# Second layer: the second product takes its first two factors in chunks 0 to 3, then 4 to 7

## The chip, the cores and the metric

The kernel runs on one core of a Trainium2 chip. The metric is the device time of one execution in microseconds. Engines are named as in the profile: PE (matrix products, with its weight loads as PEld), DVE (vector), ACT (scalar), POOL, and SP, which issues most DMAs.

## The reference

Attention with two softmaxes that are taken apart (no product of q and k), then two layers of the same shape:

```python
kv = einsum('bhsd,bhse->bhde', softmax_over_s(k), v)
x = einsum('bhsd,bhde->bhse', softmax_over_d(q), kv)     # as 4608 tokens x 512
h = x @ w_in;  x = square(maximum(h, 0)) @ w_out          # first layer, 512 -> 2048 -> 512
h = x @ w_in2; g = where(h > 0, h, exp(minimum(h, 0)) - 1)
out = g @ w_out2                                          # second layer, 512 -> 2048 -> 512
```

Everything is fp32. Each factor of a product is taken as the sum of a high and a low half (fp32r), and three of the four products of halves are computed.

## The kernel before, in words

Attention and first layer fill the first 849 us and are the same in both kernels. The change lies in `second_layer` (lines 1014 to 1077).

The second layer goes over five blocks of tokens, three with twice 512 tokens and two with twice 384 (`SIZES`); they are called wide and narrow here, and numbered 0 to 4. Both of its products are done by a scheme that replaces eight products of quarters by seven ("units" 0 to 6) of sums and differences of quarters. A block has two parts.

First product (line 871): 56 small products of six matmuls, for eight chunks m of two times 128 hidden features and seven units i each. `ORDER` (line 845) gives each a step number from 0 to 56, and after the product of a step the work put at that step is issued. Three accumulators A, B and C (`CHAIN`) hold the partial sums of a chunk; units 0, 2, 4 and 5 add into A in turn, and between them ACT (`keep_part`, line 896, and 908) or DVE (`h_part`, line 910) reads it out. Then the ELU of a row of quarters runs in five pieces: `elu_1` to `elu_3` on ACT (lines 916, 922, 927), `elu_4` and `elu_5` on DVE (931, 935). Results lie in `g2`, quarters B11, B12, B21, B22; two chunks m make one chunk pair k = 0 to 3.

Second product (line 976): 56 units u, taken two by two as pairs q = 0 to 27. `SECOND` (line 839) names the factor i and chunk j of each unit; chunks 2k and 2k+1 need the quarters of chunk pair k. Factor 4 is T3 = B22 - B12, factor 3 is T1 = B12 - B11, which is computed in place of B12. `t2_sum` (line 949, DVE) makes these differences; `d_split` (lines 956 and 957) makes a pair's high half dh on ACT and its low half dl on DVE, into three buffers each. `d_mm` then multiplies 128 x 128 pieces of dh and dl with w, in the order dh, dl, dh: 24 matmuls a pair in a wide block, 18 in a narrow one.

Each engine does its instructions in the order in which they are issued here. Splits 0, 1 and 2 are issued during the first product, split q+2 after pair q for q from 1. `put(("d", q), ...)` puts work behind pair q of the second product, `put(step, ...)` behind a step of the first. The last chunk's ELU falls on pairs 0 to 3. The weights come through a ring of 11 tiles (`w2_load`), loaded by SP in the order of use.

```python
            for q in range(NU // 2):
                d_mm(n, 2 * q)
                d_mm(n, 2 * q + 1)
                run(steps.get(("d", q), ()))
                if 0 < q < NU // 2 - 2:
                    d_split(n, q + 2)
```

Of the kernel before, what the change touches and what calls it, by code (L numbers as in the profile page):

```python
# [20 lines left out]
def tile_attention_moe_moe2(  # L21
# [714 lines left out]
    def u_out(t, i, side, half, block, m):  # L736

        o = parts_y[i][m]
        nc.vector.tensor_tensor(o, o, accs[side, m], op=ALU.add)
        nc.gpsimd.dma_start(x2d[block][2 * half + m], o)  # L740
# [95 lines left out]

    SECOND = [(i, j) for js in (range(6), range(6, 8)) for i in (4, 3) for j in js]
    SECOND += [(i, j) for i in (0, 6, 2, 1, 5) for j in range(NG)]  # L840
    SIDE = {i: (side, new) for i, side, new in SEVEN}

# [4 lines left out]
    def stream():  # L847
        for n in range(len(SIZES)):
            for _, m, i in ORDER:
                yield w2s[m][:, i]  # L850
            for i, j in SECOND:
                yield w3s[j][:, i]
# [33 lines left out]
    def take(n, m, i):  # L886
        c = CHAIN[i], m
        begin = i in (0, 1, 3)
        if begin:
            ps, tag = (psh, "ph") if i == 0 else (psa, "att")  # L890
            acc[c] = ps.tile([P, SIZES[n]], F32, tag=tag, name=f"p{n}_{m}_{i}")
        product(n, i, acc[c], begin)
# [46 lines left out]
    def quarter(name, k):  # L939
        if name == "T3":  # L940
            return g2["T3", k]
        r, side = {"B11": (0, 0), "B12": (0, 1), "B21": (1, 0), "B22": (1, 1), "T1": (0, 1), "T2": (0, 0), "T4": (1, 0)}[name]
        return g2[r, k][:, :, side]
# [7 lines left out]
    def d_split(n, q):  # L951
        i, j = SECOND[2 * q]
        x = quarter(UNITS[i], j // 2)
        hi = shifted("gh", f"dh{n}_{q}", n)
        lo = shifted("gl", f"dl{n}_{q}", n)
        nc.scalar.activation(hi, x, AF.Copy)  # L956
        nc.vector.tensor_tensor(lo, x, f32(hi), op=ALU.subtract)  # L957
        ops["d", q] = hi, lo
# [7 lines left out]
    def d_mm(n, u):  # L966
        i, j = SECOND[u]
        side, new = SIDE[i]
        w, (hi, lo) = ring.pop(0), ops["d", u // 2]
        for b, row, count in pieces2(n):  # L970
            if new and j == 0:
                y2[side, b] = psy.tile([P, count * HW], F32, tag=f"y{2 * side + b}", name=f"y2_{n}_{i}_{b}")
            for a in range(count):
                at = slice(row + a * P, row + (a + 1) * P)
                for s, x in ((0, hi), (0, lo), (1, hi)):
                    nc.tensor.matmul(  # L976
                        y2[side, b][:, a * HW : (a + 1) * HW],
                        x[:, u % 2, at],
                        w[:, s],
                        start=(new and (j, s, a) == (0, 0, 0) and x is hi),  # L980
                        stop=(j == NG - 1 and s == 1),
                        skip_group_check=True,
                    )
        w2_load()
# [16 lines left out]
    def d_out(n, i, side, half, to):  # L1001

        o = kept[i]
        for b, row, count in pieces2(n):
            c = slice(b * DM, b * DM + count * HW)
            nc.vector.tensor_tensor(o[:, c], o[:, c], y2[side, b], op=ALU.add)
            at = START[n] + to * SIZES[n] + row
            queue = nc.scalar if n == len(SIZES) - 1 and i == 4 and b else nc.sync
            queue.dma_start(
                out[at : at + count * P, half * HW : (half + 1) * HW].rearrange("(a p) c -> p a c", p=P),  # L1010
                o[:, c].rearrange("p (a c) -> p a c", c=HW),
            )

    def second_layer():


        nonlocal pool2
        for m in range(2):
            u_out(NB - 2, 4, 0, 1, NB - 2, m)
        early2.tile([P, 56], F32, tag="even", name="even")  # L1020
        layer_pool.__exit__(None, None, None)
        square_pool.__exit__(None, None, None)
        pool2 = ctx.enter_context(tc.tile_pool(name="pool2", bufs=1, reuse_waits="tile"))
        last = len(SIZES) - 1
        for n in range(last + 1):
            steps = {}

            def put(key, f, *a):
                steps.setdefault(key, []).append((f, (n, *a)))

            evict = {
                0: (keep_part, 0), 3: (keep_part, 3), 2: (keep_part, 2), 1: (h_part, 0, 0, 1, 0),
                6: (h_part, 0, 1, 6, 2), 4: (h_part, 1, 1, 4, 3), 5: (h_part, 1, 0, 5, None),
            }
            for at, m, i in ORDER:
                put(at, evict[i][0], m, *evict[i][1:])
            if n:
                put(1, lambda n: d_out(n - 1, 4, 0, 1, 0))
            for m in range(NG):
                for x, (to, f, r) in enumerate((  # L1040
                    (6, elu_1, 0), (7, elu_2, 0), (8, elu_3, 0), (9, elu_4, 0), (10, elu_5, 0), (10, elu_1, 1),
                    (11, elu_2, 1), (12, elu_3, 1), (13, elu_4, 1), (14, elu_5, 1),
                )):
                    put(7 * m + to if m < NG - 1 else ("d", (0, 0, 0, 1, 1, 1, 2, 2, 3, 3)[x]) if x else 56, f, m, r)
            for k in range(3):
                put(14 * k + 22, t2_sum, "T3", k)
                put(14 * k + 25 if k < 2 else ("d", 0), t2_sum, "T1", k)
            put(30, d_split, 0)
            put(39, d_split, 1)
            put(54, d_split, 2)  # L1050
            for q, f, *a in (
                (4, t2_sum, "T3", 3), (4, t2_sum, "T1", 3),
                (6, d_keep, 4, 0, "e"), (8, d_v), (10, t2_sum, "T2", 0), (11, t2_sum, "T2", 1),
                (12, d_keep, 0, 0, "g"), (12, t2_sum, "T2", 2), (13, t2_sum, "T2", 3), (16, d_keep, 6, 1, "g"),
                (19, t2_sum, "T4", 0), (20, d_out, 6, 0, 0, 1), (21, d_out, "v", 0, 1, 1), (22, t2_sum, "T4", 1),
                (23, t2_sum, "T4", 2), (24, t2_sum, "T4", 3), (25, d_out, 0, 1, 0, 0),
            ):
                put(("d", q), f, *a)
            if n < last:
                for q, f, a in (  # L1060
                    (6, x2_sum, "T3"), (7, x2_sum, "T1"), (9, x2_split, 0), (14, x2_sum, "T2"), (15, x2_split, 1),
                    (16, x2_split, 6), (17, x2_split, 2), (18, x2_split, 3), (25, x2_sum, "T4"), (26, x2_split, 4),
                    (27, x2_split, 5),
                ):
                    steps.setdefault(("d", q), []).append((f, (n + 1, a)))
                for k, (side, h) in enumerate(((0, 0), (1, 0), (1, 1), (0, 1))):
                    steps.setdefault(35 + 2 * k, []).append((x2_load, (n + 1, h, side)))
            for at, m, i in ORDER:
                take(n, m, i)
                run(steps.get(at, ()))  # L1070
# [6 lines that stand above are left out]
        d_out(last, 4, 0, 1, 0)  # L1077
# [6 lines left out]
    def run(steps):  # L1084
        for f, a in steps:
            f(*a)
# [3 lines left out]
    with tc.manual_schedule():  # L1090
# [107 lines left out]
        for t in range(NB):  # L1198
# [40 lines left out]
            if right:  # L1239
                steps = pair_steps(t - 1, final)  # L1240
                for u in range(NU):
                    unit(t - 1, u)
        second_layer()


# [45 lines left out]
```

## Time and profile before

| | |
|---|---|
| median of 3 runs | 1565.22 us (1564.33 to 1568.18) |
| the profiled execution | 1564.8 us, its span 1563.0 us |
| PE busy | 1534.6 us, 98% of the span |
| DVE, ACT busy | 1230.0 us (79%), 1018.9 us (65%) |
| POOL busy | 122.9 us (8%) |
| mean granted clock of PE | 0.999 of 2.4 GHz |

The span is what the trace covers. Times in the trace are microseconds from its start. A busy PE alone says that the time is PE's; the waits of PE, one by one, and the chain of work that ended last say where another engine sets it.

### The profile page before, as it was taken

The numbers are of one execution on the slowest core, as the hardware profiler recorded it, in microseconds if no ns is written. First come the engines' busy times: TensorE is split into PE (matmuls) and PEld (weight loads), VectorE is DVE, ScalarE is ACT, GpSimd is POOL, SyncE is SP. The second block draws the span as 40 slices with busy tenths as digits, with TensorE's granted clock in tenths as the row PEclk, the third lists the DMA queues.
The fourth block names the chain that finished last, engine by engine and source line by source line (L and its number), as shares of the span: only waits on it lengthen the run. The fifth ranks groups of instructions, "written<-read, shape, count | busy, mean of one in ns | idle before, by whom it ended". The sixth has DMA issues, their size and how long they took to land.

```text
span 1563.0 us, 25532 instructions
## 1 busy us (share of the span) xinstructions
PE 1534.6 (98%) x9046; PEld 1324.2 (85%) x9046; DVE 1230.0 (79%) x1807; ACT 1018.9 (65%) x1636; POOL 122.9 (8%) x194
## 2 busy tenths in 40 slices
PE   6999999999999999999999999999999999999998
PEld 4777787887878787787888889988998899999998
DVE  7998687887778887786687788678877886887885
ACT  7886655567565765656564885388538853864863
POOL 0001220032001410022201000000000000000000
PEclk9999999999999999999999999999999999999999
DMA  9867566867576775755686786767687768888876
GB/s 250 250 175 234 203 242 192 276 222 242 180 242 228 268 260 150 251 184 183 210 280 212 195 246 180 241 196 244 182 240 195 233 181 243 280 259 280 262 238 206
DMA packets 201343, 352.99 MB, mean 226 GB/s; under 512 B 20224, under 2 KB 67328, under 8 KB 201216
## 3 DMA queue, kind: packets, MB, share of 16 engines
q1 hardware_dynamic: 186672, 304.03, 64.6%
q0 software_dynamic: 14400, 47.20, 7.6%
q8 instruction: 73, 1.20, 0.3%
q14 instruction: 54, 0.44, 0.1%
q10 hardware_dynamic: 144, 0.13, 0.0%
HBM read 288.36 MB, written 62.91 MB: 225 GB/s over the span
## 4 chain that ended last, share of the span: by engine, by line
PE 79%; DVE 12%; ACT 3%; issue 2%; DMA 1%; SPq 0%; DVEq 0%; ACTq 0%
PE p L871 21%; PE y L976 18%; PE p L710 16%; PE ph L593 7%; PE ph L595 7%; PE ph L594 7%; DVE dl L957 2%; PE px L427 1%; DVE ul L698 1%; PE pk L307 1%; DVE g L935 1%; PE pt L399 1%; ACT dh L956 1%; DVE t L931 1%; DMA w<-w1s 1%
## 5 line engine op out<-in xcount | busy, mean ns | idle before, releaser
L976 PE MATMUL y<-w,dh 128*128 128x256 f32 x2016 | 359.2, 281 | 0.0
L871 PE MATMUL p<-x2h,w 128*128 128x512 f32 (+1 forms) x1120 | 321.5, 367 | 0.0
L976 PEld LDWEIGHTS y<-w,dh 128*128 128x128 f32 x2016 | 309.8, 189 | 0.1
L976 PE MATMUL y<-w,dl 128*128 128x256 f32 x1008 | 285.3, 283 | 2.9 <-DVE dl L957 2.5
L710 PE MATMUL p<-uh,w 128*128 128x512 f32 x896 | 282.7, 392 | 0.1
L593 PE MATMUL ph<-xh,wi0h 128*128 128x512 f32 x576 | 229.6, 399 | 0.1
L871 PEld LDWEIGHTS p<-x2h,w 128*128 128x128 f32 x1120 | 207.1, 188 | 26.0
L595 PE MATMUL ph<-xh,wi0l 128*128 128x512 f32 x576 | 225.4, 391 | 2.7 <-DVE wi0l L149 2.7
L594 PE MATMUL ph<-xl,wi0h 128*128 128x512 f32 x576 | 225.1, 391 | 1.3 <-DVE xl L506 1.3
L871 PE MATMUL p<-x2l,w 128*128 128x512 f32 (+1 forms) x560 | 205.7, 367 | 0.0
L710 PEld LDWEIGHTS p<-uh,w 128*128 128x128 f32 x896 | 168.3, 188 | 36.7 <-issue 1.5
L976 PEld LDWEIGHTS y<-w,dl 128*128 128x128 f32 x1008 | 189.8, 188 | 5.8 <-DVE dl L957 5.3
L956 ACT ACTIVATE dh<-g 128x1024 fp32r<-128x1024 f32 (+1 forms) x120 | 115.8, 973 | 101.3 <-PE y L976 100.1
L697 ACT ACTIVATE uh<-B 128x512 fp32r<-128x512 f32 x192 | 120.4, 631 | 93.4 <-PE p L710 69.2
L710 PE MATMUL p<-ul,w 128*128 128x512 f32 x448 | 176.5, 394 | 1.8 <-DVE ul L698 1.4
L957 DVE TENSOR_TENSOR dl<-g,dh 128x1024 fp32r<-128x1024 f32 (+1 forms) x120 | 133.8, 1115 | 42.2 <-ACT dh L956 41.8
L698 DVE TENSOR_TENSOR ul<-B,uh 128x512 fp32r<-128x512 f32 x192 | 129.6, 688 | 46.5 <-ACT uh L697 45.9
L602 ACT ACTIVATE B<-ph 128x512 f32<-128x512 f32 x128 | 76.2, 596 | 119.9 <-PE ph L595 116.2
L593 PEld LDWEIGHTS ph<-xh,wi0h 128*128 128x128 f32 x576 | 109.2, 190 | 28.2 <-issue 3.9
L595 PEld LDWEIGHTS ph<-xh,wi0l 128*128 128x128 f32 x576 | 108.3, 188 | 26.5 <-DVE wi0l L149 3.5
L594 PEld LDWEIGHTS ph<-xl,wi0h 128*128 128x128 f32 x576 | 108.5, 188 | 23.4 <-DVE xl L506 2.3
L871 PEld LDWEIGHTS p<-x2l,w 128*128 128x128 f32 x560 | 105.2, 188 | 13.0
(141 smaller groups left out, 2287.2 us busy)
## 6 DMA issues: line engine op xcount, KB each, us to landing
w<-w2s SPq DMA_DIRECT2D x280, 256.0 KB, 3.2
w<-w3s SPq DMA_DIRECT2D x280, 256.0 KB, 3.0
w<-w1s SPq DMA_DIRECT2D x224, 256.0 KB, 3.6
raw_wo<-wo_dram SPq DMA_DIRECT2D x32, 512.0 KB, 4.2
ks<-k_dram SPq DMA_DIRECT2D x32, 320.0 KB, 4.5
vr<-v_dram SPq DMA_DIRECT2D x32, 320.0 KB, 5.4
kt<-kt_dram SPq DMA_DIRECT2D x32, 288.0 KB, 4.0
q<-q_dram SPq DMA_DIRECT2D x36, 256.0 KB, 5.0
```

The source lines that it names most:

```text
L307: nc.tensor.matmul(pk[j * D : (j + 1) * D], ks[:, c, j * D : (j + 1) * D], vr[:, c, j * (D + 1) : (j + 1) * (D + 1)], start=(c == 0), stop ...
L593: nc.tensor.matmul(ph, hi[:, c], xh[p], start=(p == 0), stop=False)
L594: nc.tensor.matmul(ph, hi[:, c], xl[p], start=False, stop=False)
L595: nc.tensor.matmul(ph, lo[:, c], xh[p], start=False, stop=(p == NP - 1))
L602: nc.scalar.activation(g, ph, AF.Relu)
L697: nc.scalar.activation(hi, x, AF.Copy)
L698: nc.vector.tensor_tensor(lo, x, f32(hi), op=ALU.subtract)
L710: nc.tensor.matmul(accs[side, m], w[:, s, m], x, start=(new and (j, s) == (0, 0) and x is hi), stop=(j == NG - 1 and s == 1), skip_group_c ...
L871: nc.tensor.matmul(acc, w[:, s, c], x[:, k], start=(begin and (k, s) == (0, 0) and x is hi), stop=((k, s) == (1, 1)), skip_group_check=not ...
L956: nc.scalar.activation(hi, x, AF.Copy)
L957: nc.vector.tensor_tensor(lo, x, f32(hi), op=ALU.subtract)
L976: nc.tensor.matmul(y2[side, b][:, a * HW : (a + 1) * HW], x[:, u % 2, at], w[:, s], start=(new and (j, s, a) == (0, 0, 0) and x is hi), st ...
```

## The change

`SECOND` gives another order of the pairs. Before: T3 of k = 0, 1, 2 (pairs 0 to 2), T1 of k = 0, 1, 2 (pairs 3 to 5), T3 of k = 3, T1 of k = 3 (pairs 6, 7). After: T3 of k = 0, 1 (pairs 0, 1), T1 of k = 0, 1 (pairs 2, 3), T3 of k = 2, 3 (pairs 4, 5), T1 of k = 2, 3 (pairs 6, 7). The differences and the third split are issued at other steps.

```diff
-    SECOND = [(i, j) for js in (range(6), range(6, 8)) for i in (4, 3) for j in js]
+    SECOND = [(i, j) for js in (range(4), range(4, 8)) for i in (4, 3) for j in js]
...
             for k in range(3):
-                put(14 * k + 22, t2_sum, "T3", k)
-                put(14 * k + 25 if k < 2 else ("d", 0), t2_sum, "T1", k)
+                put(14 * k + 22 if k < 2 else ("d", 1), t2_sum, "T3", k)
+                put(14 * k + 25 if k < 2 else ("d", 3), t2_sum, "T1", k)
             put(30, d_split, 0)
             put(39, d_split, 1)
-            put(54, d_split, 2)
+            put(47, d_split, 2)
             for q, f, *a in (
-                (4, t2_sum, "T3", 3), (4, t2_sum, "T1", 3),
+                (3, t2_sum, "T3", 3), (4, t2_sum, "T1", 3),
```

The order on DVE in block 0, steps 47 to 51, before. In the names dl_2 is the low half of split 2, g the quarters, p the accumulators of the first product (p_6_0 is A of chunk 6), t either a piece of the ELU or, as t_0_2 and t_0_3, T3 of k = 2 and 3 of block 0; the last number only tells buffers apart.

```order
L910 TENSOR_TENSOR g_0_3_9416<-k_6_2_9402,p_6_3_9372 128x512
L910 TENSOR_TENSOR g_0_3_9417<-k_6_3_9381,p_6_0_9358 128x512
L931 SCALAR_TENSOR_TENSOR t_5_1_9419<-e_5_1_9405,t_5_1_9419 128x1024
L935 SCALAR_TENSOR_TENSOR g_0_2_9234<-g_0_2_9234,t_5_1_9419 128x1024
L949 TENSOR_TENSOR t_0_2_9469<-g_0_2_9234,g_0_2_9233 128x1024
L931 SCALAR_TENSOR_TENSOR t_6_0_9455<-e_6_0_9441,t_6_0_9455 128x1024
```

The same steps on DVE after the change:

```order
L910 TENSOR_TENSOR g_0_3_9416<-k_6_2_9402,p_6_3_9372 128x512
L957 TENSOR_TENSOR dl_2_9432<-g_0_0_8895,dh_2_9431 128x1024
L910 TENSOR_TENSOR g_0_3_9417<-k_6_3_9381,p_6_0_9358 128x512
L931 SCALAR_TENSOR_TENSOR t_5_1_9419<-e_5_1_9405,t_5_1_9419 128x1024
L935 SCALAR_TENSOR_TENSOR g_0_2_9234<-g_0_2_9234,t_5_1_9419 128x1024
L931 SCALAR_TENSOR_TENSOR t_6_0_9459<-e_6_0_9445,t_6_0_9459 128x1024
```

Split 2, now of T1 of k = 0, stands ahead of the eviction of p_6_0 at step 48; T3 of k = 2 has left.

The order on DVE in block 0 behind pairs 1 to 5 of the second product, before. Here g_0_2_9233 as the only name of an L949 is T1 of k = 2, and g_0_3_9416 T1 of k = 3.

```order
L957 TENSOR_TENSOR dl_3_9609<-g_0_0_8895,dh_3_9608 128x1024
L957 TENSOR_TENSOR dl_4_9644<-g_0_1_9058,dh_4_9643 128x1024
L931 SCALAR_TENSOR_TENSOR t_7_1_9640<-e_7_1_9606,t_7_1_9640 128x1024
L935 SCALAR_TENSOR_TENSOR g_0_3_9417<-g_0_3_9417,t_7_1_9640 128x1024
L957 TENSOR_TENSOR dl_5_9680<-g_0_2_9233,dh_5_9679 128x1024
L949 TENSOR_TENSOR t_0_3_9711<-g_0_3_9417,g_0_3_9416 128x1024
L949 TENSOR_TENSOR g_0_3_9416<-g_0_3_9416 128x2x512
L957 TENSOR_TENSOR dl_6_9715<-t_0_3_9711,dh_6_9714 128x1024
L957 TENSOR_TENSOR dl_7_9747<-g_0_3_9416,dh_7_9746 128x1024
```

The same place on DVE after the change:

```order
L949 TENSOR_TENSOR t_0_2_9605<-g_0_2_9234,g_0_2_9233 128x1024
L957 TENSOR_TENSOR dl_3_9608<-g_0_1_9058,dh_3_9607 128x1024
L957 TENSOR_TENSOR dl_4_9645<-t_0_2_9605,dh_4_9644 128x1024
L931 SCALAR_TENSOR_TENSOR t_7_1_9641<-e_7_1_9603,t_7_1_9641 128x1024
L935 SCALAR_TENSOR_TENSOR g_0_3_9417<-g_0_3_9417,t_7_1_9641 128x1024
L949 TENSOR_TENSOR g_0_2_9233<-g_0_2_9233 128x2x512
L949 TENSOR_TENSOR t_0_3_9679<-g_0_3_9417,g_0_3_9416 128x1024
L957 TENSOR_TENSOR dl_5_9682<-t_0_3_9679,dh_5_9681 128x1024
L949 TENSOR_TENSOR g_0_3_9416<-g_0_3_9416 128x2x512
L957 TENSOR_TENSOR dl_6_9715<-g_0_2_9233,dh_6_9714 128x1024
L957 TENSOR_TENSOR dl_7_9747<-g_0_3_9416,dh_7_9746 128x1024
```

T3 of k = 3 is followed by its own split, which is now split 5 and no longer split 6; T1 of k = 2 stands in the place of the old split 5, and T3 of k = 2 ahead of split 3.

## Rows read from the trace of the kernel before

**Rows 1.** The page's busy times: engine, busy us, share of the span, instructions.
```profile
PE 1534.6 (98%) x9046; PEld 1324.2 (85%) x9046; DVE 1230.0 (79%) x1807; ACT 1018.9 (65%) x1636; POOL 122.9 (8%) x194
```
**Rows 2.** Chain that ended last, pieces in order of time: start, length in us.
```profile
943.52 62.82 PE y L976 x527
...
1006.34 70.75 PE p L871 x312
...
1319.79 54.10 PE p L871 x312
```
**Rows 3.** Engines by stretch: length, busy us (instructions) each; PE clock, DMA share, GB/s.
```profile
920.00:944.00 24.00, 23.50 (x175) 22.31 (x174) 20.66 (x20) 16.33 (x17) 0.00 (x0) 1.00 0.70 188
```
**Rows 4.** Waits of PEld from 920 us to the end: us, times, longest.
```profile
PEld y L976 <- DVE dl L957: 5.3, 12, 0.7
```
**Rows 5.** DVE in order of time, block 0: start, us, line, out<-in [idle before, releaser].
```profile
914.98 0.69 DVE L910 TENSOR_TENSOR g<-k,p 128x512 f32<-128x512 f32 x1 [0.48 <-PE p L871]
...
925.13 1.23 DVE L957 TENSOR_TENSOR dl<-t,dh 128x1024 fp32r<-128x1024 f32 x1 [1.30 <-ACT dh L956]
...
932.80 1.22 DVE L957 TENSOR_TENSOR dl<-g,dh 128x1024 fp32r<-128x1024 f32 x1
935.16 1.23 DVE L957 TENSOR_TENSOR dl<-g,dh 128x1024 fp32r<-128x1024 f32 x1 [1.14 <-ACT dh L956]
...
938.70 1.22 DVE L957 TENSOR_TENSOR dl<-g,dh 128x1024 fp32r<-128x1024 f32 x1
939.83 1.22 DVE L949 TENSOR_TENSOR t<-g,g 128x1024 f32<-128x1024 f32 x1
...
942.24 1.23 DVE L957 TENSOR_TENSOR dl<-t,dh 128x1024 fp32r<-128x1024 f32 x1
```
**Rows 6.** ACT in order of time, block 0.
```profile
914.80 1.04 ACT L916 ACTIVATE e<-g 128x1024 f32<-128x1024 f32 x1
...
926.99 1.06 ACT L916 ACTIVATE e<-g 128x1024 f32<-128x1024 f32 x1 [0.52 <-DVE g L910]
...
941.14 1.07 ACT L956 ACTIVATE dh<-t 128x1024 fp32r<-128x1024 f32 x1 [5.07 <-DVE t L949]
```
**Rows 7.** PE in order of time, block 0.
```profile
925.67 0.28 PE L976 MATMUL y<-w,dh 128*128 128x256 f32 x1
...
943.52 0.39 PE L976 MATMUL y<-w,dl 128*128 128x256 f32 x1 [0.50 <-DVE dl L957]
```
**Rows 8.** PE in order of time, block 3.
```profile
1377.87 0.28 PE L976 MATMUL y<-w,dh 128*128 128x256 f32 x1
...
1392.13 0.39 PE L976 MATMUL y<-w,dl 128*128 128x256 f32 x1 [0.42 <-DVE dl L957]
```
**Rows 9.** ACT in order of time, block 3.
```profile
1369.91 0.83 ACT L916 ACTIVATE e<-g 128x768 f32<-128x768 f32 x1
...
1379.12 0.85 ACT L916 ACTIVATE e<-g 128x768 f32<-128x768 f32 x1 [0.56 <-DVE g L910]
```
**Rows 10.** DVE in order of time, block 3.
```profile
1378.54 0.55 DVE L910 TENSOR_TENSOR g<-k,p 128x384 f32<-128x384 f32 x1
...
1385.58 0.96 DVE L957 TENSOR_TENSOR dl<-g,dh 128x768 fp32r<-128x768 f32 x1 [1.00 <-ACT dh L956]
```
**Rows 11.** The page's DMA issues: count, KB each, us from issue to landing.
```profile
w<-w3s SPq DMA_DIRECT2D x280, 256.0 KB, 3.0
```
**Rows 12.** PE in order of time, first layer, around its one long wait.
```profile
42.23 0.39 PE L594 MATMUL ph<-xl,wi0h 128*128 128x512 f32 x1
44.94 0.50 PE L595 MATMUL ph<-xh,wi0l 128*128 128x512 f32 x1 [2.33 <-DVE wi0l L149]
...
46.82 0.63 PE L593 MATMUL ph<-xh,wi0h 128*128 128x512 f32 x1
...
50.09 0.40 PE L627 MATMUL y<-gh,wo 128*128 128x512 f32 x1
```
**Rows 13.** Engines by stretch, columns as in rows 3.
```profile
47.00:48.00 1.00, 1.00 (x4) 0.80 (x3) 0.97 (x2) 1.00 (x3) 0.00 (x0) 0.50 0.57 94
```

## The prediction

> **What bounds the kernel now.** I read the busy shares first: PE works 98% of the span [rows 1], so the time changes only where PE is made to wait, or to run slower. Then the chain of waits in order of time: the second layer alternates a first product ("PE p", 312 matmuls in 70.75 us, so 0.2268 us each; 54.10 us, 0.1734 us each, in the two narrow blocks of 384 columns) with a second product ("PE y", 527 matmuls in 62.82 us, 0.1192 us each) [rows 2]. Inside those pieces PE never stops. Between them, at the head of each second product, the chain leaves PE: in the stretch 920 to 944 PE is busy 23.50 of 24.00 us at full clock [rows 3]. The list of waits gives the whole price of these heads: weight loads of line 976 waited 5.3 us in 12 waits, all for the low half dl of a split on DVE [rows 4]. So 5.3 us is all that the change can win here, 0.34% of the time. A measurement of this kernel tells about 0.3% from no change, here 4.7 us.
>
> Why the wait arises shows in block 0. DVE works through the last ELU (L931, L935), the differences T3 and T1 (L949) and the splits (L957) one after the other. The difference T3 of k=3 starts at 939.83 and feeds ACT's dh at 941.14, then DVE's dl at 942.24 [rows 5, 6]; PE's first matmul on that dl starts at 943.52, after 0.50 us of idling [rows 7]. This is pair 6, the seventh pair. In block 3 the same matmul starts at 1392.13 [rows 8].
>
> **What the change removes and adds.** The counts are the same on every engine. Three things move.
>
> 1. *The third split, from step 54 to step 47.* It now takes T1 of k=0, ready long before. What goes is the 1.30 us for which DVE waits for this dh at 925.13 [rows 5], with an eviction and the ELU queued behind it. The first ELU of the last row (ACT, 926.99) had waited 0.52 us for that eviction, in block 3 0.56 us [rows 6, 9]. That much earlier the last ELU chain may start, no more: before it, ACT must copy the last product's result, and that waits for PE.
>
> At its new place the split costs something. On ACT dh goes in where the next ELU now starts, 914.80 [rows 6]; dl follows some 1.1 us after a dh (941.14 to 942.24 [rows 5, 6]), at 915.9. On DVE the eviction of step 48 stands behind it. It ran at 914.98 for 0.69 us [rows 5]; now it starts one dl later (1.13 us, from 938.70 to 939.83 [rows 5]), at 917.0, and ends at 917.7. The product of step 51 adds into the same accumulator, so it must wait for this read. Step 51 begins six products of six matmuls before the second product's start at 925.67 [rows 7], which is 36 times 0.2268 = 8.2 us earlier, at 917.5. PE waits 0.2 us. In the narrow blocks: dh takes the slot of 1369.91 and lasts 0.83 [rows 9], dl starts at 1370.8 and the eviction some 0.9 later, ends 0.55 after that [rows 10] at 1372.2; step 51 starts 36 times 0.1734 = 6.2 us before 1377.87 [rows 8], at 1371.6. PE waits 0.6 us. As bounds: nothing (if the accumulator were not shared) and one whole dl, 1.2 us. I take 0.2 and 0.6.
>
> 2. *T3 of k=3 is needed one pair earlier.* It was used by pair 6, and now by pair 5. What stands before it on DVE hardly changes. The old split 5 ahead of it makes room for T1 of k=2, of the same size (1.13 us from 938.70 to 939.83 [rows 5]); the second listing of the order shows it. T3 of k=2 goes in ahead of split 3, whose dl started at 932.80; but split 4 behind it was waiting for ACT anyway, 1.14 us at 935.16 and 1.00 us in block 3 [rows 5, 10], so from split 4 on DVE keeps ACT's time, and ACT is 0.52 or 0.56 us earlier. So T3 of k=3 comes 0.52 us earlier, and from it to PE nothing gets shorter (T3, dh, dl, matmul): PE can use dl at 943.52 - 0.52 = 943.00, in block 3 at 1392.13 - 0.56 = 1391.57.
>
> Due it is at the second matmul of pair 5. A pair has 24 matmuls, in narrow blocks 18. Block 0: 925.67 + 121 x 0.1192 = 940.09, so PE loses 2.9 us. Block 3: 1377.87 + 91 x 0.1192 = 1388.72, so it loses 2.85 us. A few tenths of this fall at pair 3 already, whose dl now stands behind T3 of k=2. What is late next is dl of split 6, behind T1 of k=3: by the same steps it ends about 945.2 and is due at 945.9. It holds, with 0.6 us to spare.
>
> 3. *The weights' order.* SP issues the same loads of 256 KB in the new order; one lands in 3.0 us [rows 11], and the ring holds 11, each good for 12 matmuls or 1.43 us. I count nothing; with that cover gone, each moved load could hold PE for up to 3.0 us. The accumulator of the second factor is opened one pair earlier, long after its last reader; the eviction of the first one can now run a pair earlier, which takes away the last wait of the narrow blocks (it is in the 5.3).
>
> Sum of the waits: three blocks at 2.9 + 0.2 and two at 2.85 + 0.6 make 16.2; less the 5.3 that go: **+10.9 us**.
>
> **The clock.** There is one stall of this size in the trace. PE had been dense, then stood idle for 2.33 us until 44.94 [rows 12]. After it the granted clock fell: 0.50 at 47 to 48 us, which is 1.2 instead of 2.4 GHz [rows 13]. From 46.82 to 50.09 eight matmuls lie 0.41 us apart [rows 12] where 0.2268 is the rule: 1.5 us lost. The 0.50 us stall at 943.52 cost no clock [rows 3, 7]. The new stall of a wide block is 2.9 us with a single matmul inside, longer than the one that lost the clock; that of a narrow block, about 2.3 us after the part at pair 3, is of its size. I take it that the three wide blocks lose the clock once each and the narrow ones don't: 3 x 1.5 = 4.5 us, between nothing and 5 x 1.5 = 7.5.
>
> The Trainium skill speaks to this ("TensorE: Matmul & The Clock Gate", section "Why this matters for your kernels"): it warns only of idle gaps longer than any worked out here. The trace disagrees: its gap was shorter than the page's and lost the clock. By the page nothing would be added to the waits.
>
> The sum is 10.9 + 4.5 = 15.4 us. The profiled execution took 1564.8 us; it would take 1580.2. It stands 0.4 under the median of the three runs, 1565.22, so the median becomes **1580.6 us**.
>
> **The rivals.**
>
> *The clock holds (0.30).* The waits come as summed, but no stall, or one at most, costs the clock: 1565.2 + 10.9 = 1576.1 us. For it: one stall in one trace is thin evidence, and the new stall has a matmul inside. Against it: that one stall was shorter, after dense work just as here. This is also what the skill's rule above would give.
>
> *The waits change places only (0.05).* If T3 of k=3 came 1.9 us earlier than I say (in block 0 at 937.4 instead of 939.3), PE would lose about 1.0 us a block, as it does on the mean now: 1565 us. For it: DVE has idle time in this stretch, 1.30 and 1.14 us [rows 5]. Against it: the second of these is a wait for ACT, whose own chain begins at a copy that waits for PE.
>
> *Faster (0.03).* The removed wait at 925.13 frees DVE early enough that every split is there in time, and all 5.3 us go: 1559.9 us. It decides at T3 of k=3: it must start before 936.4 in block 0, 3.4 us before its old time. Only 0.52 us of that is in the rows.
>
> *The change doesn't do what it says.* The order on DVE shows the moves; I give it nothing.
>
> **How the numbers follow.** The forecast, with two to five clock losses, has 0.60: 1579 to 1584 us. With the first rival's 0.30 and 0.02 for something else that is slower, slower by over 0.3% has 0.92; within 0.3% 0.05; faster 0.03. For the range: the low end takes the held clock without the waits at step 51 (1576.1 - 1.8 = 1574.3) and a little off each stall, 1573.5. The high end takes five clock losses (1583.6) and half a microsecond more in each block, 1586.
>
> **What would show it.** In the changed profile PE should wait for dl of pair 5 in each block, once for about 2.9 us in all (as a wait for ACT's dh and one for DVE's dl with a matmul between), and no longer at pair 6. At step 51 a matmul of line 871 should wait 0.2 and 0.6 us for DVE's line 910. ACT's dh of T3 k=3 should follow L949 at once, with DVE idle for about a microsecond before that dl. The granted clock should read 0.50 for some microseconds after the stalls of the wide blocks. The prediction is wrong if pair 5 finds its dl ready, if PE waits for weights (DMA), or if the first layer's time moves at all.

## The result, and the profile after

| | before | after |
|---|---|---|
| median of 3 runs | 1565.22 us (1564.33 to 1568.18) | 1583.38 us (1582.36 to 1586.14) |
| ratio | 1 | 1.0116 (95% interval 1.0103 to 1.0130) |
| the profiled execution, its span | 1564.8, 1563.0 us | 1582.36, 1580.6 us |

The change costs 18.2 us. The median of 1583.4 us is 2.8 above the forecast of 1580.6 and inside the range. PE still works 98% of the span and the other engines do what they did; the page's busy times answer to [rows 1]:

```profile
PE 1542.0 (98%) x9046; PEld 1328.9 (84%) x9046; DVE 1231.1 (78%) x1807; ACT 1018.8 (64%) x1636; POOL 123.2 (8%) x194
```

PE is busy 7.4 us longer with the same 9046 matmuls. That is not waiting, so part of the loss should be slower matmuls, which are looked for below. The rest is in the list of waits. Here are PE's weight loads from 851 us to the end (us in total, times, longest), which answer to [rows 4]:

```profile
PEld y L976 <- ACT dh L956: 7.4, 5, 1.6
PEld y L976 <- DVE dl L957: 6.4, 10, 1.1
PEld p L871 <- DVE g L910: 3.1, 5, 0.8
```

The second product waits 13.8 us in place of 5.3, and a wait of the first product for an eviction is new, once in each block. The list has no wait for a DMA. PE in order of time shows where pair 5 waits, in blocks 0 and 3 (start, us, line, operands [idle before, releaser]; compare [rows 7, 8]):

```profile
942.76 0.38 PE L976 MATMUL y<-w,dh 128*128 128x256 f32 x1 [1.33 <-ACT dh L956]
944.02 0.38 PE L976 MATMUL y<-w,dl 128*128 128x256 f32 x1 [0.88 <-DVE dl L957]
...
1383.10 0.45 PE L871 MATMUL p<-x2h,w 128*128 128x384 f32 x1 [0.46 <-DVE g L910]
1396.41 0.38 PE L976 MATMUL y<-w,dl 128*128 128x256 f32 x1 [0.29 <-DVE dl L957]
1402.03 0.38 PE L976 MATMUL y<-w,dh 128*128 128x256 f32 x1 [1.20 <-ACT dh L956]
1403.02 0.38 PE L976 MATMUL y<-w,dl 128*128 128x256 f32 x1 [0.61 <-DVE dl L957]
```

Block 3 has the three waits that the prediction placed: step 51, pair 3, and pair 5 in two halves around one matmul on dh. The cause stands on DVE in block 0:

```profile
930.79 1.23 DVE L931 SCALAR_TENSOR_TENSOR t<-e,t 128x1024 f32<-128x1024 f32 x1 [1.98 <-ACT e L927]
...
935.68 1.22 DVE L957 TENSOR_TENSOR dl<-t,dh 128x1024 fp32r<-128x1024 f32 x1
...
939.21 1.22 DVE L949 TENSOR_TENSOR g<-g 128x1024 f32<-128x1024 f32 x1
940.35 1.22 DVE L949 TENSOR_TENSOR t<-g,g 128x1024 f32<-128x1024 f32 x1
942.75 1.23 DVE L957 TENSOR_TENSOR dl<-t,dh 128x1024 fp32r<-128x1024 f32 x1 [1.18 <-ACT dh L956]
```

T1 of k=2 (939.21) stands ahead of T3 of k=3 (940.35), and DVE idles 1.18 us until that T3's dh is made. Earlier, before the last ELU, it idles 1.98 us.

The slower matmuls are in the chain of waits (start, length, matmuls): the piece behind pair 5's stall in blocks 0 to 2.

```profile
944.02 65.46 PE y L976 x551
...
1103.10 67.00 PE y L976 x551
...
1263.70 66.94 PE y L976 x551
```

The same 551 matmuls take 1.5 us more in blocks 1 and 2 than in block 0. The engines by stretch (columns as in rows 3) say why; the last column but two is the granted clock:

```profile
1104.00:1106.00 2.00, 2.00 (x11) 2.00 (x11) 1.93 (x3) 1.06 (x1) 0.00 (x0) 0.50 0.00 0
1264.00:1267.00 3.00, 3.00 (x17) 3.00 (x16) 2.93 (x3) 1.06 (x1) 0.00 (x0) 0.51 0.00 0
1404.00:1407.00 3.00, 3.00 (x16) 3.00 (x16) 2.53 (x3) 2.12 (x4) 0.00 (x0) 0.50 0.29 87
1527.00:1530.00 3.00, 3.00 (x16) 3.00 (x16) 1.65 (x2) 2.04 (x4) 0.00 (x0) 0.50 0.24 87
943.00:946.00 3.00, 2.12 (x17) 1.98 (x17) 3.00 (x3) 1.44 (x2) 0.00 (x0) 1.00 0.18 69
```

After the stalls of blocks 1 to 4 PE ran at 1.2 GHz for a few microseconds (rows one to four); block 0, whose stall is the same as that of block 1, kept 2.4 GHz (last row).

### The profile page after: what moved, and what is told of

Its sections match the earlier page's. It is cut to its first block, busy times and chain, and to the rows that moved or that the text cites. A ratio compares the mean times of both kernels' runs of the same rounds, so it can differ in the third digit from the quotient of the medians.

```text
span 1580.6 us, 25531 instructions
## 1 busy us (share of the span) xinstructions
PE 1542.0 (98%) x9046; PEld 1328.9 (84%) x9046; DVE 1231.1 (78%) x1807; ACT 1018.8 (64%) x1636; POOL 123.2 (8%) x194
## 4 chain that ended last, share of the span: by engine, by line
PE 77%; DVE 10%; ACT 7%; issue 2%; DMA 1%; SPq 0%; DVEq 0%; ACTq 0%
PE y L976 19%; PE p L871 17%; PE p L710 17%; PE ph L593 7%; PE ph L594 7%; PE ph L595 7%; ACT dh L956 1%; ACT e L916 1%; ACT t L922 1%; DVE dl L957 1%; PE px L427 1%; PE pk L307 1%; DVE ul L698 1%; ACT e L927 1%; PE pt L399 1%
## 5 line engine op out<-in xcount | busy, mean ns | idle before, releaser
L976 PE MATMUL y<-w,dh 128*128 128x256 f32 x2016 | 366.1, 284 | 6.4 <-ACT dh L956 6.4
L976 PEld LDWEIGHTS y<-w,dh 128*128 128x128 f32 x2016 | 315.0, 191 | 7.6 <-ACT dh L956 7.4
L931 DVE SCALAR_TENSOR_TENSOR t<-e,t 128x1024 f32<-128x1024 f32 (+1 forms) x80 | 89.2, 1114 | 42.6 <-ACT e L927 42.5
```

What stands on the lines that cost most here:

```text
L931: nc.vector.scalar_tensor_tensor(g, e, 1.0, g, ALU.add, ALU.mult)
L976: nc.tensor.matmul(y2[side, b][:, a * HW : (a + 1) * HW], x[:, u % 2, at], w[:, s], start=(new and (j, s, a) == (0, 0, 0) and x is hi), st ...
```

## The experiments

The theory: (A) T3 of k=3 comes too late for pair 5; (B) the third split at step 47 holds step 51's product by way of the eviction queued behind it; (C) the stalls cost the clock on top. The rivals: most of the loss comes from the moved split and not from the order of the pairs; the second product waits for something else of the head; what PE loses beside the waits isn't the clock's doing. The table gives medians and ratios to the kernel before on the same chip; the kernel before took 1564.40 us on the chip of e1 to e4 and 1565.29 on that of e5 to e7, so medians of different chips differ by up to about 1 us for that alone. The other columns are of the profiled execution: the waits of the weight loads of the second product (y) and of the first (p), how many blocks lost the clock, and the length of the second layer, from its first matmul (line 871) to the end of the span. Since the first layer takes up to some 3 us more or less from execution to execution, this length is the surer measure.

| kernel | us | ratio (95%) | waits, y | waits, p | blocks that lost the clock | second layer |
|---|---|---|---|---|---|---|
| before | 1565.22 | 1 | 5.3 | none | 0 | 713.5 |
| after | 1583.38 | 1.0116 (1.0103 to 1.0130) | 13.8 | 3.1 | 4 | 730.3 |
| e1_split48 | 1577.21 | 1.0082 (1.0067 to 1.0097) | 13.9 | none | 3 | 726.2 |
| e2_sums0 | 1573.41 | 1.0054 (1.0039 to 1.0069) | 9.6 | 3.1 | 2 | 722.9 |
| e3_fill | 1575.42 | 1.0069 (1.0054 to 1.0084) | 5.5 | 3.1 | 0 | 724.3 |
| e4_split54 | 1583.14 | 1.0116 (1.0092 to 1.0139) | 17.1 | none | 5 | 732.3 |
| e5_both | 1568.29 | 1.0021 (1.0012 to 1.0030) | 9.6 | none | 1 | 718.7 |
| e6_442 | 1561.09 | 0.9971 (0.9960 to 0.9981) | 2.2 | none | 0 | 710.4 |
| e7_442_dh4 | 1559.40 | 0.9962 (0.9949 to 0.9974) | 0.9 | none | 0 | 708.2 |

**The third split one step later (e1_split48).** Edit, against the changed kernel:

```diff
-            put(47, d_split, 2)
+            put(48, d_split, 2)
```

> The changed kernel with the third split one step later, at step 48, behind the eviction that it stood ahead of. Theory (the eviction of step 48 queues behind dl of split 2 and holds the product of step 51): the five waits of line 871 for DVE's line 910 (3.1 us by the weight loads) go, the waits of line 976 stay at 13 to 14 us; about 1580 us, plus or minus 1.5 for one clock loss more or less. Rival (the product of step 51 waits for something else of the head, say ACT's evictions): the waits of line 871 stay, 1583 us.

The waits of line 871 are gone, the others stay, 13.9 us: (B) stands. What a block gains shows in the chain, from one first product to the next, here blocks 1 and 2 of this kernel:

```profile
1007.67 76.20 PE p L871 x336
...
1167.92 76.19 PE p L871 x336
...
1328.10 58.29 PE p L871 x336
```

Block 1 takes 160.25 us and block 2 160.18, against 160.61 and 160.53 (1009.49 to 1170.10 to 1330.63) in the changed kernel, the clock being lost in both. So step 51 cost a wide block 0.35 us, and not the 0.51 us for which its weight load waits in the changed kernel, part of which passes while PE still works on the matmul before:

```profile
918.52 0.19 PEld L871 LDWEIGHTS p<-x2h,w 128*128 128x128 f32 x1 [0.51 <-DVE g L910]
```

The median came out 3 us under the expectation. The second layer is 4.1 us shorter than in the changed kernel: step 51 is worth 2.5 of them (three times 0.35 and twice some 0.7), and one clock loss less (block 3 kept it) 1.5. What the medians fell beyond that lies ahead of the second layer or between the chips.

**The two differences of k=2 in DVE's idle time (e2_sums0).** Edit, against the changed kernel:

```diff
-                put(14 * k + 22 if k < 2 else ("d", 1), t2_sum, "T3", k)
-                put(14 * k + 25 if k < 2 else ("d", 3), t2_sum, "T1", k)
+                put(14 * k + 22 if k < 2 else ("d", 0), t2_sum, "T3", k)
+                put(14 * k + 25 if k < 2 else ("d", 0), t2_sum, "T1", k)
```

> The changed kernel with T3 and T1 of k=2 both behind pair 0, where DVE idles 1.98 us, instead of behind pairs 1 and 3. Theory (pair 5 waits because T3 of k=3 comes too late for it): that T3 starts 1.14 us earlier in a wide block and 0.87 in a narrow one, the waits at pair 5 shrink by as much, all waits of line 976 fall from 13.8 to about 6 us; 1576 us if the clock is still lost four times, about 1570 us if the shorter stalls keep it. Rival (pair 5 waits for its buffers or for ACT's own queue): the waits stay, 1583 us.

The waits fell from 13.8 to 9.6 us, and the time by 10 us: (A) stands, the rival falls. The size was missed. The expectation's own shifts (3 x 1.14 and 2 x 0.87) make 5.2 and not the 8 that it took off, and 4.2 came. DVE in block 0 shows why:

```profile
935.17 1.23 DVE L957 TENSOR_TENSOR dl<-t,dh 128x1024 fp32r<-128x1024 f32 x1 [0.94 <-ACT dh L956]
...
937.56 1.23 DVE L935 SCALAR_TENSOR_TENSOR g<-g,t 128x1024 f32<-128x1024 f32 x1
938.82 1.23 DVE L949 TENSOR_TENSOR t<-g,g 128x1024 f32<-128x1024 f32 x1
```

T3 of k=3 starts 3.65 us after dl of split 4 (935.17 to 938.82), where it started 4.67 us after it in the changed kernel (935.68 to 940.35): 1.02 us and not 1.14, since 1.26 us lie between it and the ELU piece that it now follows and reads. The two differences take 2 x 1.14 us and the gap held 1.98, so the ELU pieces behind it moved back by the rest; that cost nothing, as DVE still waited 0.94 us for ACT's dh of split 4. The clock fell in two blocks only; twice 1.5 us and the 4.2 of waits make 7.2 of the 7.4 us by which the second layer is shorter.

**The stall filled with work (e3_fill).** Edit, against the changed kernel; the added products go to a spare accumulator and change nothing in the output:

```diff
         w, (hi, lo) = ring.pop(0), ops["d", u // 2]
+        if u == 10:
+            ps = psh.tile([P, HW], F32, tag="ph", name=f"fill{n}")
+            for _ in range(16 if n < 3 else 12):
+                nc.tensor.matmul(ps, ops["d", 4][0][:, 0, 0:P], w[:, 0], start=True, stop=True)
```

> The changed kernel with 16 (narrow blocks: 12) more matmuls of 128x256 ahead of pair 5, into a spare accumulator that nobody reads: 1.9 and 1.4 us of work inside a stall of 2.2 and 1.8 us. Theory (four of the five stalls cost the clock, some 1.5 us each): the clock stays at full speed in the second layer and the pieces of 551 matmuls all take 65.5 us; no time is added, about 1577 us. Rival (what the blocks 1 to 4 lose more than block 0 isn't the clock's doing, or the added matmuls push dl's matmul back): 1583 us or more.

PE of this kernel in order of time, block 0, and the stretches of blocks 1 and 3:

```profile
938.88 2.08 PE L973 MATMUL fill<-w,dh 128*128 128x256 f32 x16
940.80 0.28 PE L980 MATMUL y<-w,dh 128*128 128x256 f32 x1
941.64 0.39 PE L980 MATMUL y<-w,dl 128*128 128x256 f32 x1 [0.56 <-DVE dl L957]
```

```profile
1076.00:1106.00 30.00, 29.38 (x215) 27.69 (x214) 25.27 (x24) 19.00 (x22) 0.00 (x0) 1.00 0.63 168
...
1380.00:1410.00 30.00, 29.10 (x232) 28.70 (x231) 25.34 (x31) 17.80 (x24) 0.00 (x0) 1.00 0.74 221
```

The useful matmul on dl still waits for the same dl, so nothing is repaired; but the clock stays at 1.00, and blocks 1 to 3 take 159.11, 159.10 and 121.46 us in place of 160.61, 160.53 and 122.97: 1.5 us less each. That is the price of one clock loss, by itself: (C) stands. Its second layer is 6.0 us shorter (1572.2 - 847.9 against 1580.6 - 850.3, each from the first matmul of line 871), four times 1.5; the medians differ by 8.0, so up to 2 us of that is other scatter, and the median lies 1.6 us under the expectation.

**The third split back at step 54: the order of the pairs alone (e4_split54).** Edit, against the changed kernel:

```diff
-            put(47, d_split, 2)
+            put(54, d_split, 2)
```

> The changed kernel with the third split back at step 54: the new order of the pairs alone. Theory: the waits of line 871 (3.1 us) go, but the eviction of step 55 waits for dl again, the last ELU starts 0.5 us later, and each stall at pair 5 grows by as much, 2.6 us in all: within 1 us of the changed kernel if the clock falls as often, 1583 us, and 1.5 more if block 0 loses it too. Rival (most of the loss comes from the moved split, not from the order of the pairs): near 1570 us.

As expected, and as slow as the changed kernel: what line 871 no longer waits (3.1 us) comes back as waits for dl, 9.6 us in place of 6.4. It comes at pair 3 (0.81 us in place of 0.17 in block 0) and not, as expected, at pair 5. The order of the pairs with its due times makes the whole loss by itself (second layer 732.3 us, against 730.3 in the changed kernel and 713.5 before); the rival falls. All five blocks lost the clock.

**Both repairs (e5_both).** Edit: those of the first two experiments together.

> The changed kernel with both earlier edits: the third split at step 48 and the two differences of k=2 behind pair 0. Theory (the two waits add up): no wait of line 871, waits of line 976 as with the two differences moved alone, 9.6 us by the weight loads; 3 us less than that kernel, about 1570 us, so still slower than the kernel before: what is left is the order of the pairs. Rival (once the head is relieved, DVE reaches T3 of k=3 in time): waits of line 976 under 5 us and 1563 us.

The waits add up as expected: none of line 871, 9.6 us of line 976. The time is 1568.3 us, still slower than before; the second layer is 4.2 us shorter than with the differences moved alone, 2.5 of it from step 51 and 1.5 from one clock loss less. PE waits at pair 5 as in the kernel with the differences moved alone. Blocks 0 and 2 of this kernel:

```profile
938.52 0.39 PE L976 MATMUL y<-w,dh 128*128 128x256 f32 x1 [0.57 <-ACT dh L956]
939.78 0.38 PE L976 MATMUL y<-w,dl 128*128 128x256 f32 x1 [0.87 <-DVE dl L957]
...
1253.90 0.39 PE L976 MATMUL y<-w,dh 128*128 128x256 f32 x1 [0.60 <-ACT dh L956]
1255.16 0.38 PE L976 MATMUL y<-w,dl 128*128 128x256 f32 x1 [0.87 <-DVE dl L957]
```

```profile
1256.00:1258.00 2.00, 2.00 (x11) 2.00 (x11) 1.93 (x3) 1.06 (x1) 0.00 (x0) 0.50 0.00 0
```

Blocks 0, 1 and 2 have the same stall, and block 2 alone lost the clock.

**T3 of k=3 back at pair 6, the rest repaired (e6_442).** Edit, against the kernel with both repairs:

```diff
-    SECOND = [(i, j) for js in (range(4), range(4, 8)) for i in (4, 3) for j in js]
+    SECOND = [(i, j) for js in (range(4), range(4, 6), range(6, 8)) for i in (4, 3) for j in js]
...
-                (3, t2_sum, "T3", 3), (4, t2_sum, "T1", 3),
+                (4, t2_sum, "T3", 3), (4, t2_sum, "T1", 3),
```

> Early third split (T1 of k=0, at step 48), both differences of k=2 behind pair 0, but the pairs in the order T3 0, T3 1, T1 0, T1 1, T3 2, T1 2, T3 3, T1 3 (chunks 0 to 3, 4 and 5, 6 and 7): T3 of k=3 is due at pair 6 as in the kernel before. Theory (the due time of T3 of k=3 is what costs; the early split alone is a gain of half a microsecond a block): no wait in the wide blocks, under 1 us in the narrow ones, no clock loss, waits of line 976 under 2 us in place of 5.3: about 1561 us, faster than both. Rival (any early split of T1 disturbs the head): waits as before or more, 1565 us or slower.

The time came out as expected, 1561.1 us, faster than both kernels; the waits are a little over the 2 us expected, nearly all of them in the narrow blocks (1.9 us), and no block lost the clock. Waits of the weight loads in the second layer:

```profile
PEld y L976 <- DVE dl L957: 2.2, 6, 0.7
```

Against the kernel with both repairs only T3 of k=3 has moved, in its due time and in the step at which it is issued. In block 0 it starts 1.0 us later there, counted from the first matmul of the layer (849.4 to 939.07, against 847.4 to 936.09), and yet PE doesn't wait for it: the due time is what counts. It is worth 7.2 us by the medians and 8.3 us of the second layer, of which 7.4 are waits and 1.5 the clock loss of that kernel's profile (together a little more than the 8.3). The early split of T1, with T3 of k=2 behind pair 0, is worth 3.1 us of the second layer against the kernel before (the waits of 5.3 less 2.2), 4.2 by the medians, once T3 of k=3 is not pulled forward with it.

**Split 4 ahead of the last ELU pieces on ACT (e7_442_dh4).** Edit, against the last one:

```diff
+                if q == 2:
+                    d_split(n, 4)
                 run(steps.get(("d", q), ()))
-                if 0 < q < NU // 2 - 2:
+                if 0 < q < NU // 2 - 2 and q != 2:
                     d_split(n, q + 2)
```

> The same, with split 4 issued ahead of the last row's second and third ELU piece on ACT instead of behind them, since DVE waits for that dh. Theory (from split 4 on, DVE follows ACT): DVE's last ELU pieces and T3 of k=3 come up to 1 us earlier, the waits of line 976 go to near zero, about 1560 us. Rival (ACT's third ELU piece becomes the bound, as late as dh was): no change against the kernel with the same order, 1561 us.

The waits fall to 0.9 us, and DVE no longer waits for that dh. First the DVE row of the kernel before this edit, then that of this kernel, each in block 0:

```profile
934.39 1.23 DVE L957 TENSOR_TENSOR dl<-t,dh 128x1024 fp32r<-128x1024 f32 x1 [0.94 <-ACT dh L956]
```

```profile
934.74 1.22 DVE L957 TENSOR_TENSOR dl<-t,dh 128x1024 fp32r<-128x1024 f32 x1
```

1559.4 us is the fastest kernel here, 0.38% under the one before (0.26% to 0.51%). Against the last one the intervals overlap; that it is better by itself rests on the profiled executions (waits of 0.9 against 2.2 us, second layer 708.2 against 710.4).

## Why the prediction was right, point by point

**The sum of the waits was right.** Pairs 3 and 5 were put at 2.9 us in a wide block and 2.85 in a narrow one. In block 3 the weight loads wait 0.50 at pair 3, then 1.40 and 0.81 at pair 5, together 2.7:

```profile
1396.41 0.19 PEld L976 LDWEIGHTS y<-w,dl 128*128 128x128 f32 x1 [0.50 <-DVE dl L957]
...
1402.02 0.19 PEld L976 LDWEIGHTS y<-w,dh 128*128 128x128 f32 x1 [1.40 <-ACT dh L956]
1403.02 0.19 PEld L976 LDWEIGHTS y<-w,dl 128*128 128x128 f32 x1 [0.81 <-DVE dl L957]
```

The whole of line 976 is 13.8 us, forecast 14.4. The step behind it held, though the shift was a little larger: counted from the first matmul of line 976, T3 of k=3 starts 13.52 us in, where it started 14.16, in block 0 (926.83 to 940.35, against 925.67 to 939.83), and 10.64 for 11.31 in block 3. That is some 0.65 us earlier and not 0.52 or 0.56, while its due time moves by a whole pair.

**Step 51 was right in kind and nearly in size.** The first experiment gives 0.35 us in a wide block, forecast 0.2, and some 0.7 in a narrow one, forecast 0.6 (block 3's PE row shows 0.46 idle).

**The clock was mis-sized by one block and picked the wrong ones.** The step was: the three wide blocks lose it, since their stall is longer than that of [rows 12], and the narrow ones don't. Measured: blocks 1 to 4 lost it, block 0 didn't. The price of one, 1.5 us, was right. The size of the stall doesn't decide, since in four of these kernels (the changed one, e1, e2 and e5) blocks with stalls equal within 0.03 us went both ways; what does decide stays open. Nor was the one long wait of [rows 12] a fixed quantity (the trace's longer idling, 3.70 us until 10.73, lies at its start, where PE isn't dense yet): in the nine profiled executions it took 1.1 to 2.7 us. The clock fell after it where it took 2.1 us or more, and held in the others, among them the changed kernel:

```profile
43.95 0.50 PE L595 MATMUL ph<-xh,wi0l 128*128 128x512 f32 x1 [1.12 <-DVE wi0l L149]
```

**Together.** 13.8 + 2.5 (step 51: three times 0.35 and twice some 0.7; the latter is block 3's 122.97 - 120.72 us between the changed kernel and the first experiment, less the clock loss of 1.5) - 5.3 + 4 x 1.5 = 17.0 us. Measured for the second layer: 730.3 against 713.5 us (1563.0 - 849.5), 16.8. The forecast for this was 15.4. The waits were put 0.6 us too high, step 51 0.7 too low and the clock 1.5 too low, so the errors in part cancel, and the clock's term was near by luck: its count came near with the wrong blocks. What lies ahead of the second layer, which nothing touched, was 0.8 us longer in this execution. The prediction took any such move for a sign that it was wrong; that sign was too strict, since over the nine profiled executions the second layer begins between 847.4 and 850.7 us.

**The rivals.** That the clock holds fell with the stretches at 0.50. That the waits merely change places, or go, fell with pair 5: DVE's idle time was there, as the rival said (1.98 us), but ahead of the last ELU, where the moved differences didn't use it; and used (e2), it brought T3 of k=3 forward by 1.0 us a wide block, where this rival needed 1.9.

**The rule on the clock** of the Trainium skill ("TensorE: Matmul & The Clock Gate", section "Why this matters for your kernels") didn't hold here, as the prediction had it from [rows 12]: gaps shorter than those it warns of cost the clock four times in the changed kernel's profile, and with both repairs two gaps of 0.60 and 0.87 us with a matmul between were enough once.

## What to carry to other kernels

A reordering moves two things, when an operand is ready and when it is due; here the useful half (an early split of an operand that lies ready) gained 3 us of the second layer once it stood alone (e6), and the other half, a difference that became due one pair earlier while its chain stayed where it was, lost as much as the whole change (the order of the pairs alone, e4: 18.8 us of the second layer, with five clock losses). So list, for each operand of the consumer's order, the last step of its chain, and put the one that ends last as late as it goes. Count the clock with a wait of PE: the stalls at pair 5, 1.4 to 2.2 us of idling in two parts, cost it in 15 of 25 blocks of the five kernels that have them unfilled, and the single waits of up to 0.6 us in the other kernels' second layers cost it in none. Test it by filling the wait with useless matmuls: what is gained then is the clock's part.

## What the runs showed of the hardware that was not expected

Equal stalls cost the clock in one block and not in the next (changed kernel: 1.33 and 0.88 us in blocks 0 and 1 alike, and of these two the clock fell in block 1 only). Each loss cost some 1.5 us here, whether the stall was long or short (66.94 to 67.00 us for the 551 matmuls in place of 65.46 in the changed kernel, 66.95 in e5 after 0.60 and 0.87 us). Matmuls whose result nobody reads kept the clock at 1.00: 16 of them inside the stall (12 in a narrow block) made the second layer 6.0 us shorter and the median 8.0, though dl came no earlier.
